# A gated sum of two long sequence filters on one core: the last block's odd inputs turned by ScalarE and summed by DMA

## The chip, the cores and the metric

The kernel runs on one core of a Trainium2 chip. The metric is the device time of one execution in microseconds (us). The times shown are the median, lowest and highest of several executions; one further execution was recorded by the hardware profiler, and all durations below come from it. The engines are named as in the profile: PE (matrix products), PEld (PE's loading of weights), DVE (vector work), ACT (scaling, copies and functions), POOL and SP (which here mostly issue DMAs; SP's and POOL's queues are each worked off in order).

## The reference

The input `x` has 2048 steps of 1024 features; all arrays are bfloat16. Two filters run over it and are mixed by a gate per step:

```python
g = sigmoid((x * gate_w).sum(-1, keepdims=True))
# a: a complex diagonal state space (1024 states)
Lam_bar = exp(dt * Lam); B_bar = ((Lam_bar - 1) / Lam)[:, None] * Bmat
Bu = x @ B_bar.T
h[t] = Lam_bar * h[t-1] + Bu[t]
a = 2 * (h @ Cmat.T).real + x * Dskip
# b: a causal convolution over the whole sequence, per feature
kv = (4-tap shift of k) * v
y = irfft(rfft(kv, 4096) * rfft(ssm_k, 4096))[:2048] + kv * ssm_D
b = x * y
out = g * a + (1 - g) * b
```

## The kernel before

**The convolution** comes first (`b` without its gate). It works on eight chunks of 128 features. For a chunk `c`, PE makes the tap sums (`taps`) and the forward transforms of the filter (`fwd_K`, tiles `psk`) and of `kv` (`fwd_V`, tiles `psv`) as matrix products, ACT copies them out as spectra `Kh`, `Vh` (some of them lie in `BT` tiles that are not in use yet), DVE multiplies the spectra (`products`, tiles `G`, `wkh`, `t`, `BT`), and PE transforms back (`inverse`, tiles `psz`), ACT copies to `cv`, and SP writes it to a scratch in DRAM, `cv_scr`. A loop over `c` from 0 to 6 runs these as a software pipeline, two chunks deep: in step `c`, the product of chunk `c`, the inverse of chunk `c - 1`, the transforms of chunk `c + 1` and the taps of chunk `c + 2`. Before the transform of `kv` the chunk is folded (`times_v`): DVE multiplies by `v`, PE mirrors, ACT copies the mirrored part to `lo`, DVE makes the difference `ev`, and the sum is either made by DVE (`tt`) or added by a DMA that accumulates into its destination (`gather`, issued by POOL).

**The state space** works on four blocks of 512 steps (`tb`), and in each on four groups (`g`) of 256 states. A block's steps are split into even and odd ones. `Bu(i)` makes the inputs of one (block, group): two tiles `j` of 128 states, and for each 16 matmuls of `x` against `BT[g]` for the odd steps and 16 for the even ones. The odd inputs are then turned by one step's factor `lam` (a complex number per state) and added to the even ones: in `Bu_tile` by four more matmuls of 255 columns against diagonal matrices `lamd[g]` and, from the second block on, four of one column for the step carried over (`ends`). `lam_diag` makes these diagonals. `scan(tb, g)` then runs on DVE with half as many steps: it rotates the even inputs (`A`, `trn`), runs the recurrence with a real factor (`W`), rotates back to the states of the even steps (`hb`), and adds `lam * hb` to the odd inputs in place (`q`, `U`), which makes them the states of the odd steps. The tile `U` holds both halves.

**The rows** are sixteen stretches of 128 output steps, four to a block; within a block the first two take the even states `hb`, the last two the odd states `U`. `Cy_row(k)` multiplies the states with the turned output matrix `CT` (32 matmuls of 512 columns into `psy`), ACT scales by the gate (`scale_a`, to `ga`), `combine` adds `xr` by an accumulating DMA and writes the row, and then the loads of row `k + 3` are issued on SP (`pbb` from `cv_scr`, `xr` from `x`) and row `k + 2` is prepared: `scale_b` scales `pbb` by `1 - g` and `rows_` (the `Dskip` row) by `g` to `gd` on ACT, and a DMA accumulates `gd` into `pbb`. `product(k)` is DVE's `xr * pbb`. The last four rows are finished at the end, DVE taking part.

**The order** on each engine is written by hand: every instruction is issued after the one before it on its engine (`put`, line 93, which is why the profile gives L93 to nearly all of them). Generators (`step`, `run`) interleave the parts. The main loop of the state space goes over 16 scans `j`; in each, `advance(j)` runs scan `j` and starts scan `j + 1`, and then `plan[j]` names the tiles of inputs (`B8` is `Bu(8)`; `B12` to `B15` are the last block) and the rows (`C0` is `Cy_row(0)`) that follow. In the middle of each scan from `j = 3` on, `between()` runs one `product` if a row is prepared that is not yet multiplied. The rest of a `Bu` tile is held back (`late`) until the next tile's matmuls, or the middle of the next row, have been issued. In the convolution loop, some tiles of inputs are spread over the steps by `next(tiles)`; step 6 begins with tile (2, 1), that is `Bu(2)`, `j = 1`.

PSUM has four buffers (`psum`), taken in order of issue by all of these.

Of the kernel before, what the change touches and what calls it, by code (L numbers as in the profile page):

```python
# [20 lines left out]
def kernel(  # L21
# [63 lines left out]
    def ps2(shape, name):  # L85
        return psum.tile(shape, F32, name=name, tag="ps")
# [29 lines left out]
    def act(o, i, **kw):  # L116
        put("act", nc.scalar.activation, out=o, in_=i, **kw)
# [387 lines left out]
    def times_v(c):  # L505

        ks, v = kss[c], lds.pop(("v", c))
        tt(ks, ks, v.rearrange("p (b q) d -> p q b d", q=4), ALU.mult)
        yield
        lo = eo_pool.tile([128, 2, 4, 128], BF16, name="lo", bufs=2)  # L510
        act(lo, mirror(c), func=ACT.Copy)
        yield
        e = eo_pool.tile([128, 2, 4, 128], BF16, name="ev")
        tt(e, ks[:, 2:4], lo, ALU.subtract)
        if c in (1, NC - 1):
            tt(ks[:, 2:4], ks[:, 2:4], lo, ALU.add)
        else:
            gather(ks[:, 2:4], lo)
        eos["v", c] = e, ks[:, 2:4]
# [163 lines left out]
    def Bu(i):  # L683
        tb, g = order[i]
        if i in (10, 11):
            if i == 10:
                s5p["u2"] = xt_pool.tile([128, 2, 2, 2, 2, HB], BF16, name="U2", tag="xT")
            U = s5p["u2"][:, i - 10]
        else:
            home = uu[0 if i in (0, 1, 13, 14) else 1] if i < 6 or i in (13, 14) else s5p["uu"]  # L690
            U = home.tile([128, 2, 2, 2, HB], BF16, name="U")
        Us[tb, g] = U
        return [Bu_tile(tb, g, U, j) for j in range(2)]

    def Bu_tile(tb, g, U, j):
        xT = xTs[tb]
        ps = ps2([128, 2, HB], "odd"), ps2([128, 2, HB], "even")
        d = lamd[g][:, j]
        for a in (1, 0):
            for c in range(2):  # L700
                for dt_ in range(ND):
                    mm(ps[1 - a][:, c], BT[g][:, c, dt_, j * 128:(j + 1) * 128], xT[:, dt_, a * HB:(a + 1) * HB],
                       dt_ == 0 and (a == 1 or c == 0), a == 1 and dt_ == ND - 1)
            if a == 1:
                act(U[:, 1, :, j], ps[0], func=ACT.Copy)
                if j == 1 and tb < NTB - 1:
                    act(ends[:, tb % 2, g], U[:, 1, :, :, HB - 1], func=ACT.Copy)
        yield
        for k, c, o in ((0, 0, 0), (0, 1, 1), (1, 0, 1), (2, 1, 0)):
            if tb > 0:  # L710
                mm(ps[1][:, o, 0:1], d[:, k], ends[:, 1 - tb % 2, g, c, j:j + 1], False, False)
            mm(ps[1][:, o, 1:HB], d[:, k], U[:, 1, c, j, 0:HB - 1], False, k == 2)
        act(U[:, 0, :, j], ps[1], func=ACT.Copy)
        yield

    def scan(tb, g, fin):


        last = tb == NTB - 1 and g == NG - 1
        U = Us[tb, g]  # L720
        A = w2([128, 2, 2, HB], BF16, "A")
        W = None

        for js in ([slice(0, 1), slice(1, 2)] if last else [slice(0, 2)]):
            g2 = slice(2 * g + js.start, 2 * g + js.stop)
            full = [128, 2, js.stop - js.start, HB]
            Aj, Uj = A[:, :, js], U[:, 0, :, js]
            tt(Aj, bc(TC[:, g2][:, None], full), Uj, ALU.mult)
            if js.start == 0:
                yield  # L730
            b = w2([128, 2, 2, HB], BF16, "trn")[:, :, js]
            tt(b, bc(TS[:, g2][:, None], full), Uj, ALU.mult)
            if js.start == 0:
                if g == 0 and tb > 0:
                    carry(tb)
                step(fin)
            tt(Aj[:, 0], Aj[:, 0], b[:, 1], ALU.add)
            tt(Aj[:, 1], Aj[:, 1], b[:, 0], ALU.subtract)
            if W is None:
                W = w2([128, 2, 2, HB], BF16, "W")  # L740
            for j in range(js.start, js.stop):
                pi = 2 * g + j
                for c in range(2):
                    put("dve", V.tensor_tensor_scan, out=W[:, c, j], data0=bc(rv2[:, pi:pi + 1], [128, HB]),
                        data1=A[:, c, j], initial=0.0 if tb == 0 else init[tb][:, c, pi:pi + 1],
                        op0=ALU.mult, op1=ALU.add)
            if js.start == 0:
                run(fin)
                hbs[tb, g] = s5p["hb"].tile([128, 2, 2, HB], BF16, name="hb")
            hb = hbs[tb, g][:, :, js]  # L750
            Wj = W[:, :, js]
            tt(hb, bc(TC[:, g2][:, None], full), Wj, ALU.mult)
            if tb < NTB - 1:
                copy(WL[tb][:, :, g2], Wj[:, :, :, HB - 1])
            b = w2([128, 2, 2, HB], BF16, "trn")[:, :, js]
            tt(b, bc(TS[:, g2][:, None], full), Wj, ALU.mult)
            if not last:
                yield
            tt(hb[:, 0], hb[:, 0], b[:, 1], ALU.subtract)
            tt(hb[:, 1], hb[:, 1], b[:, 0], ALU.add)  # L760
            q = [w2([128, 2, 2, HB], BF16, "q") for k in range(2)]
            for k in range(2):
                for j in range(js.start, js.stop):
                    ts(q[k][:, :, j], hbs[tb, g][:, :, j], lam[:, k, 2 * g + j:2 * g + j + 1], None, ALU.mult)
            o, (q1, q2) = U[:, 1, :, js], [x[:, :, js] for x in q]
            tt(o, o, q1, ALU.add)
            tt(o[:, 0], o[:, 0], q2[:, 1], ALU.subtract)
            tt(o[:, 1], o[:, 1], q2[:, 0], ALU.add)
# [30 lines left out]
        gather(pbb, gd)  # L799

    def Cy_g(tb, tl, ps, g, last):
        X = hbs[tb, g] if tl < 2 else Us[tb, g][:, 1]
        tsl = slice(tl % 2 * 128, tl % 2 * 128 + 128)
        for j in range(2):
            for c in range(2):
                for dh in range(2):
                    mm(ps[dh], X[:, c, j, tsl], CT[2 * g + j][:, c, dh * 512:(dh + 1) * 512],
                       g == 0 and j == 0 and c == 0, last and j == 1 and c == 1)
# [93 lines left out]
    run(fold_K(1))  # L902
    fwd_V(0, (2, 3))

    old = none
    tiles = (b for i in range(6) for b in Bu(i))

    for c in range(NC - 1):
# [6 lines left out]
        if c == 0:  # L915
            p1 = products(0, 1)
            fwd_K(n, (0, 1))
            step(p0)
            run(tv)
            dg = dgs(nn, True)  # L920
            steps(p1, 2)
            step(p0)
            step(p1)
            run(p0)
            taps(nn, dg)
            step(sp)
            fwd_K(n, (2, 3))
            step(p1)
            run(sp)
            fwd_V(n)  # L930
            run(p1)
            run(fold_K(nn))
            tv = times_v(nn)
            step(tv)
            load("kn", 3)
            load("kT", 3)
            load_BT(0, 1)
            load_xT(0)
            lam_diag(0, lam_pool)
            continue  # L940
        if c == 1:
            load("v", 4)
# [12 lines left out]
            load("v", 6)  # L955
        if nn < NC:
            dg = dgs(nn)
        bu = next(tiles) if c in (4, 6) else none
        step(bu)
        fwd_K(n, (0, 1))  # L960
        step(bu)
# [12 lines left out]
        if nn < NC:  # L974
            tv = times_v(nn)
            step(tv)
        bu = [next(tiles) for _ in range({1: 1, 2: 1, 3: 1, 5: 1, 6: 2}.get(c, 0))] + [none, none]
        step(bu[0])
        fwd_V(n, (0, 1))
        if nn + 1 < NC:  # L980
# [6 lines left out]
        step(bu[0])  # L987
        step(bu[1])
        fwd_V(n, (2, 3))
        step(bu[1])  # L990
        if c == 1:
            lam_diag(1, lam_pool)
        old = tabs

    h3r.close()
# [51 lines left out]
        return wk.tile(shape, dt, name=name, tag="w2")  # L1047

    def turn_C(pi):
        m = m_pool.tile([128, 2, D], BF16, name="m")  # L1050
        for c in range(2):
            act(m[:, c], CT[pi][:, 1 - c], func=ACT.Identity, scale=mc2i[:, pi:pi + 1])
            yield
        for c, f in enumerate((c2r, mc2r)):
            ts(CT[pi][:, c], CT[pi][:, c], f[:, pi:pi + 1], None, ALU.mult)
        tt(CT[pi], CT[pi], m, ALU.add)
# [33 lines left out]


    NS = NTB * NG
    rows = dict(scaled=0, multiplied=0)

    def between():
        if rows["multiplied"] < rows["scaled"]:
            product(rows["multiplied"])
            rows["multiplied"] += 1
        yield

    def prepare():
        scale_b(rows["scaled"])
        rows["scaled"] += 1

    scans = [scan(j // NG, j % NG, between() if j > 2 else none) for j in range(NS)]

    def advance(j):
        step(scans[j])
# [13 lines left out]
    on_act += [lambda t=t: step(t) for t in turning[0:3] for _ in range(2)]  # L1122
    Bu_next(6)
    Bu_next(7)
    plan = ["B8", "B9 B10", "B11", "B12 C0", "C1", "C2", "C3", "B13", "C4 B14", "C5", "B15 C6", "C7", "C8", "C9", "C10", "C11"]
    step(scans[0])
    for j in range(NS):
        if 10 <= j < 14:
# [4 lines left out]
        on_act += [lambda t=t: step(t) for t in turning[2 * j + 3:2 * j + 5] for _ in range(2)]  # L1133
        for unit in plan[j].split():
            (Bu_next if unit[0] == "B" else Cy_row)(int(unit[1:]))
        if 0 < j < 3:
            prepare()
        if 11 <= j < 15:
            scale_b(j + 1)
# [53 lines left out]
```

## Time and profile before

| | |
|---|---|
| median of 3 executions | 419.56 us (419.29 to 421.05) |
| the profiled execution | 419.92 us, span of its instructions 418.1 us |
| PE busy | 396.8 us (95%) |
| PEld busy | 254.6 us (61%) |
| DVE busy | 385.7 us (92%) |
| ACT busy | 249.0 us (60%) |
| POOL busy | 50.2 us (12%) |
| mean granted clock of PE | 0.992 |

The profile is one execution. Busy time is the share in which an engine had an instruction at work; matmuls overlap, so a busy PE need not be at its peak. A group of instructions is named `out<-in` by the program's tiles, with the size and the number of instructions; in brackets stands the idle time of the engine just before, and the releaser, that is what ended it. "issue" is time in which the profile shows nothing that the engine waited for. Positions in time are us from the start of the span.

### The profile page before, as it was taken

To read this page: it belongs to the slowest core of one execution; us is meant where nothing else is said; L and a number is where in the kernel's file an instruction comes from. 1 tells how busy PE (TensorE), PEld (TensorE's weight loads), DVE (VectorE), ACT (ScalarE), POOL (GpSimd) and SP (SyncE) were. 2 spreads that over 40 slices of the span, in tenths; PEclk is the share of its full clock that TensorE was granted. 3 is DMA by queue.
4 is the path that set the end of the run, shared out by engine and by line. 5 is a ranking of instruction groups with operands and counts; after the bars stand their busy time and mean duration, and the time that the engine had idled before them with its cause. 6 is when DMAs were issued, how large, how long until landed. Compare 5 with 4: busy or idle time off the path is not lost.

```text
span 418.1 us, 7475 instructions
## 1 busy us (share of the span) xinstructions
PE 396.8 (95%) x2957; PEld 254.6 (61%) x2985; DVE 385.7 (92%) x635; ACT 249.0 (60%) x338; POOL 50.2 (12%) x71
## 2 busy tenths in 40 slices
PE   8899797998989898999999999999999999899995
PEld 5456364474746465676878888864476674344442
DVE  8799999999999999997999997599899978899995
ACT  4897887769797886465338685824544143555201
POOL 3011030201202020100000000102221011231200
PEclk9999999899999999999899999999999999999999
DMA  8779997898879591558957990115783453998702
GB/s 152 152 160 222 183 263 120 192 197 192 162 116 214 91 230 34 117 78 170 187 132 187 192 152 2 27 25 124 154 184 68 102 123 85 220 219 185 141 12 101
DMA packets 126005, 59.23 MB, mean 142 GB/s; under 512 B 105993, under 2 KB 112913, under 8 KB 125970
## 3 DMA queue, kind: packets, MB, share of 16 engines
q1 hardware_dynamic: 117664, 42.22, 47.4%
q0 software_dynamic: 8224, 16.52, 23.3%
q8 instruction: 23, 0.38, 0.4%
q14 instruction: 12, 0.10, 0.1%
q10 hardware_dynamic: 82, 0.02, 0.0%
HBM read 12.86 MB, written 8.39 MB: 51 GB/s over the span
## 4 chain that ended last, share of the span: by engine, by line
DVE 38%; issue 30%; PE 23%; DMA 4%; ACT 2%; POOL 1%; another core or an unknown queue 0%; DVEq 0%; POOLq 0%; SPq 0%
PE psy L93 12%; DVE BT L93 10%; DVE wkh L93 9%; DVE G L93 5%; DVE t L93 5%; PE psk L93 3%; PE psz L93 2%; PE odd L93 2%; DMA pbb<-cv_scr 2%; DVE ks L93 2%; PE taps L93 1%; PE psv L93 1%; DVE W L93 1%; PE even L93 1%; DMA ga<-xr 1%
## 5 line engine op out<-in xcount | busy, mean ns | idle before, releaser
L93 PEld LDWEIGHTS <-BT 128*128 128x128 bf16 x1024 | 100.5, 98 | 14.0
L93 PE MATMUL even<-xT,BT 128*128 128x256 bf16 x512 | 62.1, 275 | 0.0
L93 PE MATMUL odd<-xT,BT 128*128 128x256 bf16 x512 | 61.9, 275 | 0.0
L93 PE MATMUL psy<-CT,hb 128*128 128x512 bf16 x249 | 57.0, 379 | 1.6 <-DVE hb L93 1.3
L93 PE MATMUL psy<-CT,U 128*128 128x512 bf16 x251 | 56.3, 379 | 0.3
L93 PEld LDWEIGHTS <-hb 128*128 128x128 bf16 x256 | 24.7, 97 | 30.7 <-DVE hb L93 2.7
L93 PEld LDWEIGHTS <-U 128*128 128x128 bf16 x256 | 25.0, 98 | 29.8
L93 ACT ACTIVATE U<-even 128x512 bf16<-128x512 f32 x32 | 19.1, 596 | 35.5 <-PE even L93 35.5
L93 ACT ACTIVATE Vh<-psv 128x1024 bf16<-128x1024 f32 x32 | 31.0, 1036 | 11.6 <-PE psv L93 9.8
L93 PE MATMUL psz<-G,CI 128*128 128x512 bf16 x64 | 25.1, 392 | 11.9 <-DVE G L93 11.8
L93 DVE TENSOR_TENSOR_SCAN W<-rv,init,A 128x256 bf16<-128x256 f32 x48 | 32.1, 730 | 0.0
L93 PE MATMUL taps<-dg,kT 128*128 128x128 bf16 x512 | 31.8, 225 | 0.1
L93 PEld LDWEIGHTS <-kT 128*128 128x128 bf16 x512 | 30.3, 101 | 1.3 <-DMA kT<-in_B_k_dram 0.6
L93 PEld LDWEIGHTS <-SF 128*128 128x128 bf16 x192 | 18.7, 98 | 20.0 <-issue 0.8
L93 ACT ACTIVATE U<-odd 128x512 bf16<-128x512 f32 x32 | 19.0, 595 | 18.0 <-PE odd L93 16.7
L93 PE MATMUL psk<-eok,SF 128*128 128x384 bf16 (+1 forms) x126 | 29.0, 352 | 0.3
L93 POOL DMA_DIRECT2D pbb<-gd x12 | 10.3, 859 | 124.7 <-ACT gd L93 123.5
L93 PE MATMUL psz<-G,SI 128*128 128x512 bf16 x64 | 25.0, 391 | 0.0
L93 DVE TENSOR_TENSOR U<-U,q 128x512 bf16<-128x512 bf16 (+2 forms) x51 | 23.5, 488 | 0.6
L93 ACT ACTIVATE cv<-psz 128x1024 bf16<-128x1024 f32 x16 | 16.5, 1029 | 11.5 <-PE psz L93 8.9
L93 POOL DMA_DIRECT2D G<-wkh x8 | 9.7, 1218 | 106.3 <-DVE wkh L93 106.3
L93 ACT ACTIVATE ga<-psy,gcols 128x1024 bf16<-128x1024 f32 x8 | 8.9, 1114 | 22.5 <-PE psy L93 22.5
(166 smaller groups left out, 749.9 us busy)
## 6 DMA issues: line engine op xcount, KB each, us to landing
G<-wkh POOLq DMA_DIRECT2D x6, 768.0 KB, 7.8
cv_scr<-cv SPq DMA_DIRECT2D x16, 256.0 KB, 2.7
v<-in_B_v_dram SPq DMA_DIRECT2D x3, 1024.0 KB, 10.8
pbb<-cv_scr SPq DMA_DIRECT2D x12, 256.0 KB, 3.2
xr<-in_A_x_dram SPq DMA_DIRECT2D x12, 256.0 KB, 5.0
pbb<-gd POOLq DMA_DIRECT2D x12, 256.0 KB, 3.4
ga<-xr POOLq DMA_DIRECT2D x8, 256.0 KB, 3.4
out_dram<-ga SPq DMA_DIRECT2D x8, 256.0 KB, 3.3
```

The costliest lines, as they stand in the source:

```text
L93: i = f(*a, **kw)
```

## The change

Six things are done.

- **Factor diagonals by ScalarE:** `lam_diag` for groups 0 and 1, in the convolution loop, runs on ACT instead of DVE.
- **One state tile over two chunks:** `Bu(2)`, `j = 1`, is begun in step 5 instead of step 6: its odd half (16 matmuls, the copy and `ends`) comes before the last two transforms `fwd_V` of step 5, its even half and its diagonals stay in step 6.
- **The fold of chunk 7** takes the accumulating DMA instead of DVE's addition.
- **The last block's odd inputs** (`B12` to `B15`) get a path of their own, `Bu_last`: the odd half is kept with two more columns per row (258 instead of 256), the second of which holds the step carried over; ACT multiplies the shifted odd inputs by the factor's parts into a tile `Q` (one instruction of 512 and two of 256 columns per tile), and two accumulating DMAs per `Bu` add `Q` to the even half. The 8 diagonal matmuls per tile are gone. `Q` shares the buffers of `m`, the tile of `turn_C`.
- **Rows multiplied in their own step:** `between(j)` runs `product(k)` in the scan whose plan names `Ck`, instead of as early as a row is prepared. That is the same scan for rows 0 to 3, and one later for rows 4 to 11; scan 7 has none, scan 15 has one.
- **`prepare()`** runs after `plan[0]` and `plan[1]` instead of after `plan[1]` and `plan[2]`.

```diff
 def times_v(c):
-        if c in (1, NC - 1):
+        if c == 1:
             tt(ks[:, 2:4], ks[:, 2:4], lo, ALU.add)
         else:
             gather(ks[:, 2:4], lo)
...
 def Bu(i):
-            U = home.tile([128, 2, 2, 2, HB], BF16, name="U")
-        Us[tb, g] = U
-        return [Bu_tile(tb, g, U, j) for j in range(2)]
+            U = home.tile([128, 2 * (4 * HB + 4)], BF16, name="U")
+            if i >= 12:
+                V_, O_ = U[:, 0:4 * HB], U[:, 4 * HB:]
+                V_ = V_.rearrange("p (c j t) -> p c j t", c=2, j=2)
+                O_ = O_.rearrange("p (c j t) -> p c j t", c=2, j=2)
+                Us[tb, g] = V_, O_[:, :, :, 2:]
+                Q = m_pool.tile([128, 2, 2, 2, HB], BF16, name="Q", tag="m")
+                return [Bu_last(tb, g, V_, O_, Q, j) for j in range(2)]
+            U = U[:, 0:8 * HB].rearrange("p (a c j t) -> p a c j t", a=2, c=2, j=2)
+        Us[tb, g] = U[:, 0], U[:, 1]
+        return [Bu_tile(tb, g, U, j, (i, j) == (2, 1)) for j in range(2)]
...
+    def Bu_last(tb, g, V_, O_, Q, j):
+        xT, pi = xTs[tb], 2 * g + j
+        if j == 0:
+            act(O_[:, :, :, 1], ends[:, 1 - tb % 2, g], func=ACT.Copy)
+        for a, o in ((1, O_[:, :, j, 2:]), (0, V_[:, :, j])):
+            ps = ps2([128, 2, HB], ("even", "odd")[a])
+            for c in range(2):
+                for dt_ in range(ND):
+                    mm(ps[:, c], BT[g][:, c, dt_, j * 128:(j + 1) * 128], xT[:, dt_, a * HB:(a + 1) * HB],
+                       dt_ == 0, dt_ == ND - 1)
+            act(o, ps, func=ACT.Copy)
+            if a == 1:
+                for k, c, o, f in ((0, slice(0, 2), slice(0, 2), lam[:, 0]), (1, 0, 1, lam[:, 1]), (1, 1, 0, mlam)):
+                    act(Q[:, k, o, j], O_[:, c, j, 1:1 + HB], func=ACT.Identity, scale=f[:, pi:pi + 1])
+        yield
+        if j == 1:
+            for k in range(2):
+                gather(V_, Q[:, k])
+        yield
...
-            lam_diag(0, lam_pool)
+            lam_diag(0, lam_pool, True)
...
-        bu = next(tiles) if c in (4, 6) else none
+        bu = next(tiles) if c == 4 else ahead if c == 6 else none
...
+        if c == 5:
+            bu[1] = ahead = next(tiles)
...
         step(bu[1])
         fwd_V(n, (2, 3))
-        step(bu[1])
+        if bu[1] is not ahead:
+            step(bu[1])
         if c == 1:
-            lam_diag(1, lam_pool)
+            lam_diag(1, lam_pool, True)
...
-    def between():
-        if rows["multiplied"] < rows["scaled"]:
-            product(rows["multiplied"])
-            rows["multiplied"] += 1
+    def between(j):
+        for unit in plan[j].split():
+            if unit[0] == "C":
+                product(int(unit[1:]))
         yield
...
-        if 0 < j < 3:
+        if j < 2:
             prepare()
```

The plan itself is unchanged:

```python
plan = ["B8", "B9 B10", "B11", "B12 C0", "C1", "C2", "C3", "B13", "C4 B14", "C5", "B15 C6", "C7", "C8", "C9", "C10", "C11"]
```

More of the change, by code (lines that the diff above doesn't have):

```diff
@@ L690, in Bu, with Bu_tile @@
             home = uu[0 if i in (0, 1, 13, 14) else 1] if i < 6 or i in (13, 14) else s5p["uu"]
-            U = home.tile([128, 2, 2, 2, HB], BF16, name="U")
-        Us[tb, g] = U
-        return [Bu_tile(tb, g, U, j) for j in range(2)]
-    def Bu_tile(tb, g, U, j):
+            U = home.tile([128, 2 * (4 * HB + 4)], BF16, name="U")
[9 more added lines that the diff above has]
+        return [Bu_tile(tb, g, U, j, (i, j) == (2, 1)) for j in range(2)]
+    def Bu_tile(tb, g, U, j, halved):
         xT = xTs[tb]
-        ps = ps2([128, 2, HB], "odd"), ps2([128, 2, HB], "even")
+        ps = []
         d = lamd[g][:, j]
         for a in (1, 0):
+            ps.append(ps2([128, 2, HB], ("even", "odd")[a]))
             for c in range(2):
@@ L707, in Bu_tile @@
                     act(ends[:, tb % 2, g], U[:, 1, :, :, HB - 1], func=ACT.Copy)
+                if halved:
+                    yield
         yield
@@ L714, in Bu_tile @@
         yield
+    def Bu_last(tb, g, V_, O_, Q, j):
[16 more added lines that the diff above has]
+                gather(V_, Q[:, k])
+        yield
     def scan(tb, g, fin):
         last = tb == NTB - 1 and g == NG - 1
-        U = Us[tb, g]
+        Ve, Uo = Us[tb, g]
         A = w2([128, 2, 2, HB], BF16, "A")
@@ L726, in scan @@
             full = [128, 2, js.stop - js.start, HB]
-            Aj, Uj = A[:, :, js], U[:, 0, :, js]
+            Aj, Uj = A[:, :, js], Ve[:, :, js]
             tt(Aj, bc(TC[:, g2][:, None], full), Uj, ALU.mult)
@@ L764, in scan @@
                     ts(q[k][:, :, j], hbs[tb, g][:, :, j], lam[:, k, 2 * g + j:2 * g + j + 1], None, ALU.mult)
-            o, (q1, q2) = U[:, 1, :, js], [x[:, :, js] for x in q]
+            o, (q1, q2) = Uo[:, :, js], [x[:, :, js] for x in q]
             tt(o, o, q1, ALU.add)
@@ L801, in Cy_g @@
     def Cy_g(tb, tl, ps, g, last):
-        X = hbs[tb, g] if tl < 2 else Us[tb, g][:, 1]
+        X = hbs[tb, g] if tl < 2 else Us[tb, g][1]
         tsl = slice(tl % 2 * 128, tl % 2 * 128 + 128)
@@ L903 @@
     fwd_V(0, (2, 3))
-    old = none
+    old = ahead = none
     tiles = (b for i in range(6) for b in Bu(i))
@@ L1049, in turn_C @@
     def turn_C(pi):
-        m = m_pool.tile([128, 2, D], BF16, name="m")
+        m = m_pool.tile([128, 2, D], BF16, name="m", tag="m")
         for c in range(2):
@@ L1092 @@
     NS = NTB * NG
-    rows = dict(scaled=0, multiplied=0)
-    def between():
-        if rows["multiplied"] < rows["scaled"]:
-            product(rows["multiplied"])
-            rows["multiplied"] += 1
+    plan = ["B8", "B9 B10", "B11", "B12 C0", "C1", "C2", "C3", "B13", "C4 B14", "C5", "B15 C6", "C7", "C8", "C9", "C10", "C11"]
+    rows = dict(scaled=0)
+    def between(j):
+        for unit in plan[j].split():
+            if unit[0] == "C":
+                product(int(unit[1:]))
         yield
@@ L1103, in prepare @@
         rows["scaled"] += 1
-    scans = [scan(j // NG, j % NG, between() if j > 2 else none) for j in range(NS)]
+    scans = [scan(j // NG, j % NG, between(j)) for j in range(NS)]
     def advance(j):
@@ L1124 @@
     Bu_next(7)
-    plan = ["B8", "B9 B10", "B11", "B12 C0", "C1", "C2", "C3", "B13", "C4 B14", "C5", "B15 C6", "C7", "C8", "C9", "C10", "C11"]
     step(scans[0])
```

## The prediction, made before the changed kernel was run

> **What bounds the kernel now.** I read the sums per stretch first, then the chain of waits where it changes engine, then each engine's timeline there. Every instruction carries line L93 (the issue helper), so tiles name the work.
>
> In the sums (columns: stretch, length, busy us of PE, PEld, DVE, ACT, POOL with counts, granted clock, DMA share, GB/s) the bound changes from stretch to stretch:
>
> ```profile
> 48.00:167.00 119.00, 109.90 (x839) 68.69 (x847) 118.66 (x112) 94.81 (x135) 18.75 (x23) 0.99 0.83 165
> 167.00:193.00 26.00, 25.66 (x185) 17.48 (x189) 23.72 (x21) 13.89 (x20) 1.20 (x1) 1.00 0.52 97
> 217.00:364.00 147.00, 145.36 (x1114) 101.78 (x1120) 129.09 (x279) 77.67 (x103) 15.45 (x18) 1.00 0.56 114
> 364.00:414.00 50.00, 49.56 (x226) 22.36 (x230) 47.05 (x108) 15.83 (x15) 8.56 (x10) 1.00 0.62 135
> ```
>
> DVE has no idle time in the convolution loop (118.66 of 119.00); PE has none after 167. From 193 to 217 DVE's last products are one run (193.44 to 216.5) and PE waits 0.59 for them. So before 167 an edit counts by DVE time, from 167 to 193 by PE time, and after 217 by PE time unless DVE's scans come late. They do once; PE's timeline in row 8:
>
> ```profile
> 356.97 5.34 PE L93 MATMUL psy<-CT,hb 128*128 128x512 bf16 x24
> 363.58 1.69 PE L93 MATMUL psy<-CT,hb 128*128 128x512 bf16 x6 [1.27 <-DVE hb L93]
> ```
>
> DVE's lateness comes from the row products, scans 3, 10 and 11 in its timeline:
>
> ```profile
> 266.40 0.69 DVE L93 TENSOR_TENSOR xr<-xr,pbb 128x1024 bf16<-128x1024 bf16 x1 [7.47 <-DMA pbb<-gd]
> ...
> 343.77 0.69 DVE L93 TENSOR_TENSOR xr<-xr,pbb 128x1024 bf16<-128x1024 bf16 x1 [2.70 <-issue]
> ...
> 357.16 0.69 DVE L93 TENSOR_TENSOR xr<-xr,pbb 128x1024 bf16<-128x1024 bf16 x1 [3.52 <-issue]
> ```
>
> With 0.16 and 1.14 at scans 5 and 6 that is 15.0 us of DVE standing in a product for its gather.
>
> **Part 1, the convolution loop.** The two lam_diag sets leave DVE: each lies in one run, 48.80 to 49.78 and 73.27 to 74.24, so 0.98 and 0.97 us, all on DVE's path. ACT takes six 128x128 scalings each: the same set on ACT ran 221.66 to 223.51, 1.85 us. In c=0 it has room: ACT ends hr at 47.9 and its next tile is ready at 49.75. In c=1 it delays cv from about 73.3 to 76.0, and its buffer is wanted by PE only at 78.1; without that cover it would cost up to 2. DVE then wants the V spectrum of c=3 at 95.8, when ACT has it at 96.1: 0.3 may go. I take 1.8 of 1.95.
>
> The odd half of tile (2,1), 16 matmuls, 1.75 us, moves from c=6 ahead of the last two V transforms of c=5. PE idles 1.62 there before 167.18 (waiting for DVE's G), so it costs 0.17 on PE; the V copies end at 168.45 by the old clock, and DVE wants them at 168.17, 0.3 that DVE can afford, since in c=6 PE is late. It takes 1.75 out of 167 to 193. The 0.69 us addition of c=7, now a gather, saves nothing: DVE waits 2.58 for Vh afterwards. The gather is issued near 174 and needs under 5 us where its neighbours took 3.3 to 5.3; its reader comes at 181.4.
>
> Sum at 193, kept at 217: 1.8 - 0.17 + 1.75 = 3.4 us earlier, on PE and DVE alike.
>
> **Part 2, the rows.** The first prepare moves a scan earlier: scaling and gd (2.2 us of ACT) come near 245.6 instead of 260.6. ACT's slack to PE's next buffer there is 0.95 us a tile with 1.0 of gap beside it; I take 0.25 of PE lost. Product 0 is then ready near 251.5, before DVE wants it at 258.9, and the 7.47 us go. What is late next is product 2: its pbb is scaled only after row 0's evacuation. Row 0's matmuls ended at 283.5 and the product ran at 290.53, 7.0 us later by ga, pbb, gd and the gather. DVE without the stall would be there at 282.9, so it waits again, now tied to PE: through products 2 and 3 it stands where PE stands. From product 4 on each product is one scan later. Products 4, 6 and 7 were ready at 307, 326.6 and 343.7; earlier by as much as PE is (4.2 to 5.9), that is 303, 322 and 338, while DVE, with 9.7 to 10.2 us per scan from product 3 on, arrives at 316.6, 336 and 346. The later rows have at least 6. So the 2.70 and 3.52 go. Scan 7 has no product: DVE gains 0.61 there and gives it back in scan 15. Combine 4 waits 2 us more and holds the POOL queue (the gather of row 6 behind it), which has 13 us.
>
> **Part 3, the last block.** Eight tiles lose 8 matmuls each, 0.54 us a tile in every PE timeline (207.18 to 207.72): 4.32 us of PE. ACT gains per tile one 128x512 and two 128x256 scalings. The trace has neither; between 128x128 back to back (0.29) and 128x1024 (1.04) they come to 0.61 + 0.40 + 0.40 = 1.4 us (0.9 if all three cost as the smaller row, 3.1 if as the larger). Tile work on ACT is then 2.4 us against PE's 3.49, and the filler scalings end before B12; beyond 3.49 it would hold PE. The gather pairs: the second waits for the first's landing, so POOL is held 0.86 + 3.4 + 0.86 = 5.1 us (9 with the longest landing, 7.1). The pair of B12 comes at 273 and ga of row 0 is wanted at about 280: hidden; the others have more room. V is read by scans 12 to 15, 60 us later.
>
> The padded odd half is read and written by three DVE additions per scan (0.68, 0.42, 0.42). 128x1024 in rows of 256 out of 512 (trn<-TCS,U) also takes 0.684, so steps cost nothing; the 4-byte offset no row shows. Bounds: 0, or the rate of an addition fed from PSUM (1.22 for 1024): about 1.2 us a scan. I take 0.
>
> [...] The trace first: POOL's issues of pbb<-gd took 856/856/896 ns (min/median/max), and DVE's three U additions took 1.48 us with one beside them (309.17) as without (252.74). [...]
>
> **The sum.** Through products 2 and 3 DVE is tied to PE: 3.4 - 0.25 + 1.08 (B12) = 4.2. Row 4 then needs hb of scan 7, which DVE gives 4.2 + 0.61 = 4.8 earlier; PE would be there 5.3 earlier and waits 0.6 (so of B13's 1.08 about half is lost). B14 and B15 add 2.16: 7.0 at row 8. There hb of scan 11 comes at about 353, PE wants it at 355.3, and the 1.27 go: 8.3. DVE ends scan 15 at about 396 against 398.6 for PE's last quarter of rows. ACT's evacuation of rows 10 and 11, which the last rows' buffers wait for, moves with PE and keeps its 2 to 3 us.
>
> The profiled execution took 419.92 us (span 418.1 and 1.8 around it); the median of three runs is 419.56, 0.36 less. 419.9 - 8.3 = 411.6 by the profile; against the median 411.3.
>
> **Rivals.**
> 1. The early part is not gained: ACT, loaded with the diagonals and the early odd tile, delivers V spectra late, and 193.44 stays. For: ACT has 94.81 of 119. Against: its copies wait for PE every cycle. 4.9 left: 414.7. Chance 0.12.
> 2. The product chain stays DVE's limit beyond product 3 (late pbb loads, since out, load and gather follow each other). Then scan 11 is only 4.8 earlier and PE waits at row 8: 414.8. It decides if product 7 comes over 8 us later than I have it. Chance 0.10.
> 3. The padded additions run at the slow rate: 4.8 us over scans 12 to 15, DVE ends at 400.5, PE waits about 1.8: 413.1. Chance 0.06. DVE blocked by the gathers' issues belongs beside it: 6 issues of 0.86 before scan 11, 5.2 us, hb at 358: 414.0. Chance 0.03. [...]
> 4. Slower: weights read from the padded rows. Rows 14 and 15 load 64 weights from them, hidden as long as a load is under the 216 ns between matmuls. At twice that interval each costs 216 more, 13.8 in all: 425. It decides from about (8.3 + 2.1) / 64 + 216 = 380 ns a load. Against: loads from kT start at 1, 2 or 3 elements off and took 101 ns. Chance 0.05.
> 5. No net change, because PE's clock falls more often. It stood at 0.50 from about 203 to 206, after 96 one-column matmuls, and cost some 1.8 us; four such would eat the gain. For: PE's idle of 2.70 before 72.27 was followed by 0.50 too. Against: no wait becomes longer, and that one falls to 1.7, a length that was followed by full clock at 143.69. Chance 0.06: 419.
>
> [...]
>
> **How the numbers follow.** Forecast 0.58: 411.3. Low end: without the wait at row 4 (0.6), the 0.25 and one clock dip (1.8) it would be 408.7; I say 409.0. High end 415.5 takes in rivals 1 to 3; rivals 4 and 5 are out. A measurement of this kernel can tell about 0.5%, 2.1 us, from no change. Faster: 0.58 + 0.12 + 0.10 + 0.09 = 0.89, of which I give 0.02 to slower for what I do not see: 0.87; same 0.06; slower 0.07.
>
> **What would show it.** Right: no wait of xr in scans 3, 10 and 11, but one of 6 to 7 us in scan 5 and about 1 in scan 6; PE at the last psz about 3.4 earlier; no even<-U,lamd rows for the last block; PE waiting under 1 us for hb in row 4 and not at all in row 8; Q rows of 0.4 to 0.7 us. Wrong: G<-Kh,Vh of the last chunk at 193 still, U additions above 0.75, PE waiting for hb in row 8, weight loads of U above 110 ns, or POOL holding ga of row 0 behind a U<-Q.

## The result, and the profile after

The changed kernel takes 412.99 us (median of 4 executions, 412.28 to 413.69), the kernel before 419.63 us beside it (419.29 to 421.05): ratio 0.9835, 95% interval 0.9807 to 0.9864. Its profiled execution took 413.16 us, span 411.4 (before: 418.1). The forecast was 411.3 in a range of 409.0 to 415.5.

The sums per stretch of the changed kernel, in the same columns and stretches as before, with 193 to 217 added (busy us of PE, PEld, DVE, ACT, POOL with counts, granted clock, DMA share, GB/s):

```profile
48.00:167.00 119.00, 112.27 (x874) 70.77 (x873) 118.46 (x102) 98.48 (x148) 18.76 (x23) 1.00 0.83 165
167.00:193.00 26.00, 26.00 (x187) 17.20 (x186) 24.62 (x20) 15.55 (x21) 2.10 (x2) 1.00 0.70 133
193.00:217.00 24.00, 21.75 (x261) 17.60 (x259) 23.86 (x31) 8.35 (x19) 0.00 (x0) 0.93 0.99 165
217.00:364.00 147.00, 145.58 (x1072) 99.93 (x1071) 133.58 (x291) 88.26 (x130) 24.00 (x28) 1.00 0.67 135
364.00:414.00 50.00, 42.99 (x200) 19.27 (x197) 39.38 (x88) 14.72 (x14) 6.91 (x8) 0.98 0.54 126
```

DVE is still full in the loop (118.46 of 119.00), with 102 instructions instead of 112; ACT carries 3.7 us more there. From 217 to 364 ACT has 10.6 us more (mostly the `Q` scalings), POOL 8.6 more (6.8 of it the eight gathers of 0.86), and PE is busy for 145.58 of 147.00; the 1.42 left is the wait of row 4 shown below. The row to look at is the third: PE is busy for only 21.75 of 24.00.

PE's timeline of the changed kernel, at the last inverse (the first three rows) and at rows 4 and 8 of the output; in brackets the wait and what ended it:

```profile
212.38 0.39 PE L93 MATMUL psz<-G,CI 128*128 128x512 bf16 x1 [2.25 <-DVE G L93]
...
212.82 0.44 PE L93 MATMUL psz<-G,CI 128*128 128x512 bf16 x1
213.05 0.63 PE L93 MATMUL psz<-G,SI 128*128 128x512 bf16 x1
...
314.34 1.90 PE L93 MATMUL psy<-CT,hb 128*128 128x512 bf16 x8 [1.42 <-DVE hb L93]
...
351.57 13.98 PE L93 MATMUL psy<-CT,hb 128*128 128x512 bf16 x64
```

The same place of the kernel before:

```profile
216.54 0.39 PE L93 MATMUL psz<-G,CI 128*128 128x512 bf16 x1 [0.59 <-DVE G L93]
```

The last inverse starts 4.16 us earlier, more than forecast. But PE had stood 2.25 us for it instead of 0.59, and right behind it matmuls take 0.63 instead of 0.38: half clock, from 213.0 to 216.4. The sums of that stretch, and of the half clock that the kernel before has earlier (the eighth number is the granted clock, 0.50 in both):

```profile
213.00:216.40 3.40, 3.40 (x15) 1.60 (x14) 3.37 (x9) 0.97 (x2) 0.00 (x0) 0.50 0.00 0
```

```profile
203.00:206.40 3.40, 3.40 (x18) 2.42 (x16) 3.40 (x4) 0.81 (x2) 0.00 (x0) 0.50 1.11 147
```

The next block's matmuls start at 218.01 against 220.54, so 1.6 of the 4.16 are gone again. Then row 4 waits 1.42 for `hb`; row 8 (351.57) runs its 64 matmuls without a break. The last row ends at 406.99 against 413.83.

DVE's timeline of the changed kernel, the last chunk's first product and then the row products of scans 3, 5 and 6:

```profile
189.29 2.29 DVE L93 TENSOR_TENSOR G<-Kh,Vh 128x4096 bf16<-128x4096 bf16 x1 [1.28 <-ACT Vh L93]
...
256.33 0.68 DVE L93 TENSOR_TENSOR xr<-xr,pbb 128x1024 bf16<-128x1024 bf16 x1
...
287.45 0.69 DVE L93 TENSOR_TENSOR xr<-xr,pbb 128x1024 bf16<-128x1024 bf16 x1 [7.32 <-DMA pbb<-gd]
...
298.70 0.69 DVE L93 TENSOR_TENSOR xr<-xr,pbb 128x1024 bf16<-128x1024 bf16 x1 [1.46 <-issue]
```

The wait of 7.47 at product 0 is gone and stands at product 2, as 7.32; those of 2.70 and 3.52 are gone for good. The groups of the new operations (duration in ns: min/median/max) and DVE's additions into the tile:

```profile
L93 ACT ACTIVATE Q<-U,lam x16: 492/608/724, 268.1 to 338.1; 128x512 bf16<-128x512 bf16 x8, 128x256 bf16<-128x256 bf16 x8
L93 ACT ACTIVATE Q<-U,mlam x8: 492/493/494, 269.1 to 338.5; 128x256 bf16<-128x256 bf16 x8
L93 POOL DMA_DIRECT2D U<-Q x8: 856/856/856, 274.4 to 344.4; - x8
```

In the last block DVE's three additions into `U` take 1.48 us (at 384.84), as before on the unpadded tile.

**The account** in the profile, in us earlier than before: 0.45 at start-up, in front of everything that was changed; 3.70 in the loop; 1.62 lost to the half clock; 1.08 from B12; 1.08 from B13 less 1.45 for the wait of row 4 (1.42) and the restart behind it; 2.16 from B14 and B15; 1.44 from row 8. 0.45 + 3.70 - 1.62 + 1.08 - 0.37 + 2.16 + 1.44 = 6.84, which is the last row's 413.83 - 406.99.

### The profile page after: what moved, and what is told of

Read it like the earlier page. It is cut to its first block, busy times and chain, and to the rows that moved or that the text cites. A ratio compares the mean times of both kernels' runs of the same rounds, so it can differ in the third digit from the quotient of the medians.

```text
span 411.4 us, 7426 instructions
## 1 busy us (share of the span) xinstructions
PE 390.8 (95%) x2921; PEld 249.2 (61%) x2921; DVE 382.8 (93%) x622; ACT 263.1 (64%) x378; POOL 58.0 (14%) x80
## 4 chain that ended last, share of the span: by engine, by line
DVE 42%; PE 39%; issue 9%; DMA 4%; ACT 4%; ACTq 0%; POOL 0%; DVEq 0%; SPq 0%; POOLq 0%
PE psy L93 19%; DVE BT L93 9%; DVE wkh L93 8%; PE psk L93 4%; DVE t L93 4%; PE even L93 4%; DVE G L93 4%; DVE W L93 4%; PE odd L93 3%; PE psz L93 3%; DVE CT L93 2%; PE psv L93 2%; DVE A L93 2%; PE taps L93 2%; DVE trn L93 2%
## 5 line engine op out<-in xcount | busy, mean ns | idle before, releaser
L93 PE MATMUL even<-xT,BT 128*128 128x256 bf16 x512 | 61.1, 273 | 0.0
L93 PE MATMUL taps<-dg,kT 128*128 128x128 bf16 x512 | 30.3, 220 | 0.0
L93 PEld LDWEIGHTS <-kT 128*128 128x128 bf16 x512 | 29.1, 98 | 0.9 <-DMA kT<-in_B_k_dram 0.2
L93 PE MATMUL psk<-eok,SF 128*128 128x512 bf16 (+1 forms) x128 | 29.4, 352 | 0.0
L93 POOL DMA_DIRECT2D pbb<-gd x12 | 10.6, 885 | 113.8 <-PE even L93 71.5
L93 ACT ACTIVATE pbb<-pbb,omg 128x1024 bf16<-128x1024 bf16 x12 | 13.7, 1143 | 16.0 <-DMA pbb<-cv_scr 6.6
```

The costliest lines, as they stand in the source:

```text
L93: i = f(*a, **kw)
```

## The experiments

Twelve runs were made in three groups, each on one chip, with the kernel before among them (its medians: 420.14, 419.71 and 421.07). Two questions led: is each part worth what the sum gave it, and where did the 1.5 us go by which the profile stays behind the sum's 8.3?

### First group: each part alone

**The changed kernel again.** 

> The changed kernel as it is, beside the others on the same chip. My account of its profile: 6.7 us of span gained, of which 3.7 in the convolution loop, 0.45 at the start (other DMA times), 1.7 lost again to half-clock TensorE behind the last inverse transform, and 4.3 among the rows and the last block. Expected 413.0 us again; a profile without the half-clock stretch at 213 to 216 would be about 1.7 us shorter.

Measured: 413.87 us (412.43 to 414.02), ratio 0.983 (0.9803 to 0.9856). PE waits 1.07 in row 4, and the half clock follows the last inverse again (granted clock 0.74 from 212.5 to 219). This execution has a second stretch of half clock, from 47.6 to 51.0 (its mean granted clock is 0.992, that of the first profile 0.995), and reaches the last inverse at 213.57 instead of 212.38.

**The loop undone**: diagonals on DVE, tile (2, 1) whole in step 6, the fold of chunk 7 added by DVE.

```diff
-        if c == 1:
+        if c in (1, NC - 1):
...
-            lam_diag(0, lam_pool, True)
+            lam_diag(0, lam_pool)
...
-        bu = next(tiles) if c == 4 else ahead if c == 6 else none
+        bu = next(tiles) if c in (4, 6) else none
...
-            lam_diag(1, lam_pool, True)
+            lam_diag(1, lam_pool)
```

> The convolution loop as before (diagonals of groups 0 and 1 on DVE, tile (2,1) whole in step 6, DVE's addition for chunk 7); rows and last block as changed. Theory A (the loop's 1.95 + 1.75 pass to the end, and the changed kernel pays 1.7 for a half-clock stretch that before lay under DVE's last products): the loss is 3.7 - 1.7 = 2.0, 415.0 us. Theory B (the half-clock stretch has nothing to do with it and stays): 3.7, 416.7 us. Theory C (the loop gives nothing, V spectra late): 413.0 us.

Measured: 415.72 us (414.77 to 417.13), ratio 0.9884 (0.9856 to 0.9912), 1.9 above the changed kernel. PE's timeline of this kernel at the last inverse:

```profile
216.06 0.39 PE L93 MATMUL psz<-G,CI 128*128 128x512 bf16 x1 [2.25 <-DVE G L93]
```

216.06 is 3.68 later than 212.38, as much as the 1.95 of the diagonals and the 1.75 of the tile together (the two were not undone apart). At the end 3.0 are left in the profile (span 414.4), since PE's wait in row 4 is then 0.79 instead of 1.42. So the loop's gain is real, and the rival that it would be worth nothing falls. The wait of 2.25 and the half clock behind it (matmuls of 0.63 us from 216.96 on) are there without the loop's edits too; they don't come from this part. So theory A has its time (1.9 for 2.0) by luck: the half clock that it takes away is still there. The medians differ by less than the two profiles, 1.9 against 3.0; the profile of the changed kernel in this group has the second stretch of half clock, which the profile here has not.

**The last block undone**: its inputs turned by the 64 diagonal matmuls, nothing else.

```diff
-            if i >= 12:
+            if i >= 99:
```

> The last block's odd inputs by the 64 diagonal matmuls again; the rest as changed. Theory A (PE's 0.54 us a tile count except where PE waits in row 4 for the scan that is tied to row 0): 4.32 less about 1.1 of B13's, 3.2 us more, 416.2 us, and the wait in row 4 falls from 1.42 to about 0.35 us. Rival (PE is the bound throughout): 4.3 more, 417.3 us. Rival (DVE is the bound behind row 0): under 1 us more.

Measured: 415.51 us (414.24 to 417.94), ratio 0.9891 (0.9858 to 0.9923), 1.6 above the changed kernel. From the last inverse to the end of the span it takes 201.6 us, the changed kernel 199.0. The 4.32 us of matmuls shrink to 2.6 mostly because PE no longer waits in row 4 (1.42 in the changed kernel): what PE gained ahead of row 4 was partly stood off there. Two things take the wait away here, more work on PE and a product 3 without a wait; this run doesn't separate them.

**The rows undone**: products as early as a row is prepared, `prepare()` after `plan[1]` and `plan[2]`.

```diff
-            if unit[0] == "C":
-                product(int(unit[1:]))
+        if rows["multiplied"] < rows["scaled"]:
+            product(rows["multiplied"])
+            rows["multiplied"] += 1
...
-        if j < 2:
+        if 0 < j < 3:
```

> Products as early as a row is prepared and prepare after plan 1 and 2, as before; loop and last block as changed. Theory A (products 7 and 8 wait again in scans 10 and 11, 1.6 and 2.4 us, and row 8 waits about 1.6 us for hb): 1.9 us more, 414.9 us. Rival (DVE has slack behind row 4, so the order does not matter): 413.0 us. Rival (the 15 us of waits come back in full): over 418 us.

Measured: 415.61 us (413.85 to 418.01), ratio 0.9883 (0.9851 to 0.9914), 1.7 above the changed kernel. DVE's timeline of this kernel has the old wait at product 0:

```profile
263.37 0.69 DVE L93 TENSOR_TENSOR xr<-xr,pbb 128x1024 bf16<-128x1024 bf16 x1 [7.42 <-DMA pbb<-gd]
```

and PE's timeline has both waits for `hb`, in row 4 and in row 8:

```profile
313.58 1.90 PE L93 MATMUL psy<-CT,hb 128*128 128x512 bf16 x8 [1.10 <-DVE hb L93]
...
357.38 8.81 PE L93 MATMUL psy<-CT,hb 128*128 128x512 bf16 x39 [1.23 <-DVE hb L93]
```

So the wait of row 8 belongs to the rows' order, as forecast, and it stands even when PE comes sooner. The price, 1.7 by the medians, is less sure: the interval just touches the changed kernel's, and the profiled execution is the fastest of the six (413.85). In this execution the half clock lies earlier, as in the kernel before: the sums of 198.9 to 202.3 (granted clock 0.50), and PE's timeline at the last inverse, where PE then waits only 0.67:

```profile
198.90:202.30 3.40, 3.40 (x29) 2.46 (x26) 3.40 (x3) 0.24 (x2) 0.00 (x0) 0.50 1.26 141
```

```profile
213.57 0.39 PE L93 MATMUL psz<-G,CI 128*128 128x512 bf16 x1 [0.67 <-ACT U L93]
```

Where it lies, under DVE's products or behind the wait, is a matter of the execution, not of the edits: this kernel differs from the changed one only behind 217.

### Second group: the order of the rows, and the half clock

**The early `prepare()` alone undone.**

```diff
-        if j < 2:
+        if 0 < j < 3:
```

> Only the first two prepares one scan later, as before; all else as changed. Theory A (DVE is tied to PE by products 2 and 3, so removing the 7.47 us wait of product 0 only moved it to scan 5): product 0 waits about 7.5 us in scan 3 again, product 2 hardly waits, and the time stays 413.0 us. Rival (the early prepare is what let DVE run ahead): 3 us or more lost, 416 us.

Measured: 413.54 us (412.45 to 414.35), ratio 0.9837 (0.98 to 0.9873): nothing lost. DVE's timeline of this kernel, scans 3 and 5:

```profile
263.90 0.69 DVE L93 TENSOR_TENSOR xr<-xr,pbb 128x1024 bf16<-128x1024 bf16 x1 [7.40 <-DMA pbb<-gd]
...
287.62 0.68 DVE L93 TENSOR_TENSOR xr<-xr,pbb 128x1024 bf16<-128x1024 bf16 x1
```

The wait is back at product 0, and product 2 has none. DVE stands about 7.4 us once, in scan 3 or in scan 5; preparing earlier only chooses where. What helps is that products 4 to 11 come a scan later (the run with the rows undone has the same early wait and, besides, the one of row 8).

**Products 2 and 3 a scan later** as well: row 2's matmuls in scan 5, its evacuation, write and the prepare in scan 6, row 3 likewise in 6 and 7.

```diff
-    plan = [..., "C1", "C2", "C3", "B13", ...]
+    plan = [..., "C1", "M2", "T2 M3", "T3 B13", ...]
...
-        if unit[0] == "C":
+        if unit[0] in "CT":
...
+        rest(k)
+    def rest(k):
```

> Products 2 and 3 one scan later still (scans 6 and 7), with the rest of rows 2 and 3 (combine, loads, prepare) behind them; all else as changed. Theory A (the tie is the gather of rows 2 and 3 that DVE stands for in scans 5 and 6): both waits, 7.3 and 1.5 us, go, DVE is some 9 us ahead at row 4, PE's wait of 1.42 us there goes and all of B13's matmul time counts: 1.4 us less, 411.6 us. Rival (combine 2 and 3 come late and the rows' loads behind them make a new wait): 413 us or more.

Measured: 412.34 us (410.01 to 412.71), ratio 0.9798 (0.9762 to 0.9834). No product waits long, and PE's timeline of this kernel shows row 4 unbroken:

```profile
307.44 7.07 PE L93 MATMUL psy<-CT,hb 128*128 128x512 bf16 x31
```

About 1.2 us are won beside the kernel with the later prepare on the same chip; the intervals overlap, and in this profile the half clock lies at 198.9 to 202.3 (16 matmuls of `odd` take 3.49 us there instead of 1.91), ahead of the last inverse, so that the two profiles differ in the clock too.

**Nine unused matmuls** (128x512, of constants, into a buffer that nobody reads) in PE's wait ahead of the last inverse.

```diff
+        warm = ps2([128, 2, 512], "warm")
+        for _ in range(9):
+            mm(warm[:, 0], SF[:, 0, 0:128], SF[:, 0], True, True)
         run(back)
```

> Nine matmuls of 512 columns whose result is not used, issued on PE ahead of the last inverse transform; all else as changed. Theory A (the half-clock stretch follows PE's wait of 2.25 us for DVE's G and costs 1.7 us on PE's path): the wait is filled, the stretch does not come there, 1.7 us less, 411.3 us. Rival (the stretch has its place for another reason): 413.0 us, or more by what the extra matmuls overshoot, up to 0.3 us.

Measured: 410.91 us (410.15 to 411.29), ratio 0.9774 (0.9741 to 0.9806). PE's timeline of this kernel:

```profile
210.19 2.10 PE L93 MATMUL warm<-SF 128*128 128x512 bf16 x8
212.60 0.39 PE L93 MATMUL psz<-G,CI 128*128 128x512 bf16 x1 [0.31 <-DVE G L93]
212.83 0.38 PE L93 MATMUL psz<-G,SI 128*128 128x512 bf16 x1
213.04 0.38 PE L93 MATMUL psz<-G,CI 128*128 128x512 bf16 x1
```

The inverse starts no earlier (212.60), but runs at full clock throughout (granted clock 1.00 from 212 to 217). Row 4 doesn't wait either: product 3 came without one. So this run can't say how much of the gain is the clock's.

**Both of these together.** 

> Both of the last two. Theory A: the gains add, since one is ahead of row 0 and the other behind it: 3.1 us less than the changed kernel, 409.9 us. Rival (PE, faster ahead of row 0, waits for DVE elsewhere): 411.3 to 411.6 us.

Measured: 411.2 us (409.74 to 413.28), ratio 0.979 (0.9752 to 0.9828). From the last inverse to the end it takes 195.8 us, exactly as with the matmuls alone: the two remove the same wait of row 4 and don't add. The profiled execution (413.0) reaches the last inverse only at 215.44, after stretches of half clock at 12.1 and 49.6, in parts of the kernel that no edit here touches (its mean granted clock is 0.992, in the profile of the matmuls alone 1.00).

### Third group: is it the clock, and why does row 4 wait?

**The changed kernel on the third chip.** 

> The changed kernel unaltered, on the same chip as the three below. All theories: 412.3 to 414.0 us, with PE waiting 0.7 to 1.5 us for hb in row 4, as in its earlier profiles.

Measured: 412.39 us (412.04 to 413.51), ratio 0.9807 (0.9782 to 0.9831). In the profiled execution PE waits the same 2.25 us ahead of the last inverse, and no half clock follows. PE's timeline, the last inverse and row 4:

```profile
213.58 0.39 PE L93 MATMUL psz<-G,CI 128*128 128x512 bf16 x1 [2.25 <-DVE G L93]
...
313.56 1.90 PE L93 MATMUL psy<-CT,hb 128*128 128x512 bf16 x8 [1.06 <-DVE hb L93]
```

The sums of 212.5 to 218 here (the eighth number is the granted clock):

```profile
212.50:218.00 5.50, 4.42 (x28) 2.44 (x29) 5.46 (x14) 1.73 (x3) 0.00 (x0) 1.00 0.48 161
```

and in the changed kernel's first profile, with the same wait:

```profile
212.50:218.00 5.50, 5.50 (x24) 2.48 (x23) 5.43 (x14) 1.56 (x2) 0.00 (x0) 0.69 0.20 78
```

So the wait alone doesn't bring the half clock in every execution. Why it came in the first profile and not here was not shown.

**The nine matmuls beside it.** 

> The nine unused matmuls in PE's wait ahead of the last inverse, again, now beside the changed kernel on one chip. Theory (the half-clock stretch behind that wait costs some 1.7 us of PE): at least 1.7 below the changed kernel, 410.5 to 411.5, no half clock behind the last inverse's start. Rival (the earlier difference was between chips): within 0.8 us of the changed kernel.

Measured: 411.24 us (410.35 to 411.51), ratio 0.9769 (0.9746 to 0.9793). That is 1.15 below the changed kernel, between what was expected of the theory (1.7) and of the rival (0.8). The pair of profiles doesn't price the clock: neither has half clock behind the last inverse (granted clock 1.00 from 212.5 to 218 in both), and the 0.9 us between their spans (410.6 and 409.7) is PE's wait in row 4, 1.06 and none. All its 14 executions lie from 412.04 to 414.02, all 11 with the matmuls alone from 410.15 to 411.51; how much of this is the clock and how much row 4 is not shown for executions without a profile.

**The load of `pbb` ahead of the earlier row's write** on SP instead of behind it.

```diff
         Cy(k // NG, k % NG)
+        pbb = load_p(k + 3) if k + 3 < NT - 4 else None
         combine(k)
         if k + 3 < NT - 4:
-            loads(k + 3)
+            loads(k + 3, pbb)
```

> Each row's pbb load is issued on SP ahead of the earlier row's write instead of behind it; nothing else. Theory A (product 3 is late because its pbb load is issued late, behind row 0's write, and then lands slowly): ACT scales pbb of row 3 right behind ga of row 1 (near 288.1 instead of 290.6), product 3 runs without a wait in scan 6, PE's wait in row 4 falls from 1.4 to below 0.6, and the time is 0.8 to 1.4 below the changed kernel. Rival B (product 3 waits for ACT and the gather anyway): wait of row 4 stays at 0.7 to 1.5, time within 0.5 of the changed kernel. Rival C (the earlier load collides with the gathers of the last block and of ga): ga or U<-Q land above 5 us and the row-4 wait grows.

Measured: 411.26 us (411.13 to 413.06), ratio 0.9781 (0.9755 to 0.9807). ACT's timeline of this kernel, row 1's evacuation and row 3's scaling:

```profile
288.37 1.11 ACT L93 ACTIVATE ga<-psy,gcols 128x1024 bf16<-128x1024 f32 x1 [3.72 <-PE psy L93]
289.38 1.14 ACT L93 ACTIVATE pbb<-pbb,omg 128x1024 bf16<-128x1024 bf16 x1
```

and of the changed kernel:

```profile
286.98 1.12 ACT L93 ACTIVATE ga<-psy,gcols 128x1024 bf16<-128x1024 f32 x1 [3.72 <-PE psy L93]
290.57 1.15 ACT L93 ACTIVATE pbb<-pbb,omg 128x1024 bf16<-128x1024 bf16 x1 [2.47 <-DMA pbb<-cv_scr]
```

SP's timeline has the load itself, here and in the changed kernel:

```profile
258.42 0.38 SPq L93 DMA_DIRECT2D pbb<-cv_scr  x1
```

```profile
284.77 0.34 SPq L93 DMA_DIRECT2D out_dram<-ga  x1
285.22 0.64 SPq L93 DMA_DIRECT2D pbb<-cv_scr  x1
```

The load no longer stands behind the write, which waits for row 0, and is issued 27 us sooner. The 2.47 us in which ACT stood for it are gone, and with them product 3's wait and PE's wait in row 4, whose 32 matmuls run in one piece:

```profile
308.97 7.17 PE L93 MATMUL psy<-CT,hb 128*128 128x512 bf16 x32
```

So row 4 waited because row 3's `pbb` was loaded late. The gain, 1.1, lies within the 0.8 to 1.4 expected, though the intervals overlap. Of the six times four lie at 411.13 to 411.28, two at 413.03 and 413.06, 1.8 apart. The profiled execution is one of the two, with the wait of 2.25 and the half clock behind it; its clock is 0.72 from 212.5 to 218:

```profile
212.50:218.00 5.50, 4.24 (x19) 2.02 (x20) 5.46 (x15) 1.56 (x2) 0.00 (x0) 0.72 0.31 109
```

```profile
213.76 0.39 PE L93 MATMUL psz<-G,CI 128*128 128x512 bf16 x1 [2.25 <-DVE G L93]
```

That the other four ran at full clock there is inferred from their times; they have no profile.

**Both.** 

> Both edits: the load ahead and the nine unused matmuls. Where the row-4 wait was already gone with the matmuls alone (as in their first profile), the load adds nothing: 410.5 to 411.2, the same as the matmuls alone within 0.5. If that was an accident of the execution, the load takes the rest: up to 1.4 below the matmuls alone where their profile shows a row-4 wait.

Measured: 410.97 us (410.41 to 411.31), ratio 0.9766 (0.974 to 0.9791). Row 4 and the last inverse cost nothing more. It can't be told from the matmuls alone, which in both their profiles had no wait in row 4 either: there the load of `pbb` reached ACT 4.0 and 4.2 us after its issue instead of 5.3, and why it came sooner is open. With the matmuls, the load, or both, the median is 1.1 to 1.4 us below the changed kernel on this chip; the 95% intervals overlap with the changed kernel's and lie far below the kernel before.

The stretch from the last inverse to the end of the span takes both prices apart, since start-up and loop lie ahead of it:

| profile | half clock behind the last inverse | PE's wait in row 4 | from the last inverse to the end, us |
|---|---|---|---|
| changed kernel | yes | 1.42 | 199.0 |
| changed kernel again | yes | 1.07 | 198.6 |
| changed kernel, third chip | no | 1.06 | 197.0 |
| load first | yes | none | 197.5 |
| nine matmuls, third chip | no | none | 196.0 |
| nine matmuls and load first | no | none | 195.8 |

So the half clock costs 1.7 us (197.5 against 195.8), and row 4 costs its wait (197.0 against 196.0).

## Why the prediction was right, and where it was off

- **The loop.** 3.70 instead of 3.4. The 0.17 on PE and the 0.15 for a late V spectrum, both taken as possible losses, didn't come: DVE's products are 1.96 earlier from c=2 on (0.45 of start-up taken off), and the odd tile gave its whole 1.75. Undoing this part put back 3.68. Rival 1 is out.
- **"Against: no wait becomes longer" (rival 5).** This step failed. PE's wait ahead of the last inverse grew from 0.59 to 2.25. In the kernel before, half clock from about 203 to 206 had slowed PE while DVE's products had still 10 us to run; the stretch cost PE's slack, not time, and I priced it at 1.8 as if it cost time. Without it PE came early and waited longer; in the two profiles that have the half clock there (rows undone, products 2 and 3 later) the wait is 0.67 and 0.66. In this execution the half clock fell behind the wait, where PE is the bound: 1.62 us. The other half of the step held: the wait before 72.27 (now 70.84) fell to 1.72, and full clock followed (granted clock 1.00 from 70.84 to 77.6). The low end's "one clock dip (1.8)" less was wrong for the same reason: that dip was already free.
- **ACT's early prepare, 0.25 of PE.** Cost nothing: no matmul from 240 to 250 waits.
- **The wait moves to product 2 (6 to 7) and product 3 (about 1).** 7.32 and 1.46. Right in kind; product 3 was the term mis-sized. I took it to follow PE, but it followed the load of `pbb`, which ACT could scale only 5.35 us after its issue (285.22 to 290.57), where it took 3.7 in the profile with the last block undone (286.60 to 290.27). The load ahead of the write showed it. Whether the load collides with the gather of row 2 stays open: in six profiles with 5.2 to 5.4 us it was issued 1.66 to 1.68 behind that gather, in three with 3.7 to 4.2 it was 1.79 to 2.12.
- **0.6 of wait in row 4.** 1.42, where under 1 was the sign of being right: by 0.85 of product 3 (it came 2.76 earlier where PE was 3.61 earlier; 0.53 of this was there at product 2) and because PE's distance to DVE differed. Forecast at row 4: 4.8 earlier, measured 3.24. From this 4.8: - 1.62 (clock) - 0.85 (product 3) + 0.45 (start-up) + 0.3 (loop) + 0.25 (ACT) = 3.3.
- **After row 4.** B14 and B15 gave 2.16 and row 8 gave 1.44 with PE's restart (forecast 1.27). Right; so 8.3 became 6.84, and the difference lies at row 4 and before. The time fell into the range in part by luck: the 0.45 of start-up belongs to the execution, not to an edit, and sets off part of the half clock that wasn't foreseen.
- **The unknown costs.** The `Q` rows show 0.72 and 0.49, forecast 0.61 and 0.40; but back to back they overlap, and a tile's three take 1.43 of ACT (268.08 to 269.51), forecast 1.4, all under PE's 3.49. Padded additions: 0 extra, as taken. Weights from padded rows: 98 ns a load, so rival 4 is out. POOL: the second gather waits 2.73 for the first, and `ga` of row 0 goes out at 281.48, on time. Rival 3 is out in both forms: the padded additions ran at the usual rate, and no run shows DVE blocked by a gather's issue. The eight issues of `U<-Q` took 856 ns each, and DVE's three additions into `U` took 1.48 us with one of them beside (278.05, the issue at 277.99; 315.71, the issue at 315.68) as without (384.84).
- **The product chain (rival 2).** Right up to product 3 only, by another cause (the load, not products 4 to 7); scan 11 came in time.

## What to carry to other kernels

Before pricing a slow stretch as a loss, look at what else ran beside it. Here the half clock from 203 to 206 lay under DVE's products and cost nothing at the end; in six profiles without it there PE waited 2.25 us instead of 0.59 ahead of the last inverse, and in the changed kernel's first profile half clock followed that wait, where it cost 1.62 us. When a wait is moved to another place in the order, ask what feeds the next instruction of that kind; here the next one waited for a load queued behind a write, and the load issued ahead of the write took 1.1 us off the median. A wait of PE of known place and length can be filled with matmuls that nobody reads, if the buffer and the queue allow it; here nine of them went into the wait of 2.25 us, and no half clock followed at the last inverse in any of the four profiles that have them.

## What the runs showed of the hardware

- The half clock (granted clock 0.50) came in stretches of about 3.4 us: from 73.3 to 76.7 and from 203.0 to 206.4 in the kernel before, from 213.0 to 216.4 in the changed kernel, from 198.9 to 202.3 with the rows undone. In the one at 213.0 a matmul of 512 columns took 0.63 us, at full clock 0.38 to 0.39. The sums of the first stretch in the kernel before:

```profile
73.30:76.70 3.40, 3.40 (x10) 1.21 (x8) 3.40 (x9) 2.60 (x5) 0.00 (x0) 0.50 0.98 217
```

- What followed a wait of PE differed for waits of like length. The wait of 2.25 us ahead of the last inverse was followed by half clock in five profiles (the changed kernel, the loop undone, the last block undone, the early prepare undone, load first) and by full clock in one (the changed kernel on the third chip). In the kernel before, half clock followed a wait of 2.70 (72.27) and full clock one of 2.48 (47.81); in the changed kernel full clock followed one of 2.49 (47.35). Behind the waits of 1.57 to 1.72 in the loop of these two kernels the clock was full each time. What decides was not shown.
- The same load from DRAM, row 3's `pbb` of 256 KB, took from issue to ACT's reading it 3.7 to 5.4 us in nine profiles; the gather issued ahead of it was at most 0.46 us nearer in the slow cases.
- Half clock also came with work that had no gap, the 96 one-column matmuls of 2.54 to 2.56 us. In three profiles (the kernel before, the rows undone, products 2 and 3 later) the 16 matmuls of `odd` right behind them took 2.69, 3.48 and 3.49 us, in ten others 1.91. What decides was not shown here either. PE's timeline of the kernel before, ahead of the stretch at 203.0:

```profile
199.62 2.54 PE L93 MATMUL p<-gwb,xT 128*128 128x1 bf16 x96
202.02 2.69 PE L93 MATMUL odd<-xT,BT 128*128 128x256 bf16 x16
```
